# One fused attention and mixer kernel: batch 0's values cast whole into the hidden tile's space, its opening chain redealt over the engines, and batch 1's loads held back

## The chip, the core and the metric

The kernel runs on one core of a Trainium2 chip. Its time is the device time of one execution in microseconds, and lower is better. Five engines work side by side on a core: TensorE (PE in the profile) multiplies matrices, VectorE (DVE) and ScalarE (ACT) do element-wise work, GpSimd (POOL) does some casts and issues part of the DMA transfers, and SyncE (SP) issues the other transfers. Each engine runs its instructions in the order in which the program lists them, and semaphores hold an instruction until what it needs is there.

## The reference

The first half is a linear attention whose features are a ReLU times a cosine and a sine of the position. The second half is a mixer with a low-rank token part and a wide channel part.

```python
# q, k, v: (8 batches, 8 heads, 576 positions, 64)
phi(x) = concatenate([relu(x) * cos_w, relu(x) * sin_w], axis=-1)   # 128 features
kv  = einsum('bhsf,bhsd->bhfd', phi(k), v)
z   = sum(phi(k), axis=2)
num = einsum('bhsf,bhfd->bhsd', phi(q), kv)
den = einsum('bhsf,bhf->bhs', phi(q), z)[..., None] + 1e-06
x   = (num / den), heads side by side           # (8, 576, 512)
h   = x.transpose(0, 2, 1) @ U @ V              # U: 576 x 32, V: 32 x 576
u   = x + h.transpose(0, 2, 1)
out = u + relu(u @ w_ch1) @ w_ch2               # 512 -> 2048 -> 512
```

## The kernel before

The 576 positions of a batch lie in five chunks, `c` = 0 to 4: four of 128 positions and a tail of 64. Inputs come in as 32-bit floats (`qst`, `kst`, `vst`, one set for all batches) and are cast to bf16 for TensorE. The order of all work is written out by hand, engine by engine; nothing is planned by a scheduler. From the second batch on, attention work is dealt into slots beside the channel matmuls of the batch before. Batch 0 has nothing to hide behind, and its opening is the part that the change touches.

**The opening of batch 0** goes as follows. SyncE loads q, k and v of batch 0, then q of batch 1 into the same staging tiles as soon as they have been read, then k and v of batch 1. GpSimd loads U and V, the four slices of `w_ch1` (`w1_load`, L98) and later those of `w_ch2` (`w2_load`, L104). TensorE runs matmuls on zeros first (`keep_warm`, L195), then transposes q's features (`qtr_mm`, L366), sums k's features to z (`z_mm`, L892, one column for each head), and enters `first_chain` (L942).

**`first_chain`** works in two halves of four heads. VectorE has cast v to bf16 into `v_ext` (`v_block`, L278), and GpSimd the tail of v into `v_tl`. `kv_unit` (L315) multiplies k's features with v, with 65 columns for each head, the last one a column of ones. ScalarE casts its result to `kv`. `den_mm` (L900) makes the denominators from z, one column for each chunk and head, and `recip` (L402) inverts them on VectorE. `xh_mm` (L911) makes the numerators of one chunk and four heads, and `xh_norm` (L920) multiplies them on VectorE with the inverse and writes `x_bf`, or `x_tl` for the tail. `a_mm` (L436) makes the low-rank product `A` in two halves, each from four heads, and ScalarE casts both. `open_mm` (L935) and `uTd_mm` (L529) build the transposed u in four blocks, and `uTd_evac` (L526) casts each to `uT`. The first channel matmuls (`g1_main`, L541) read `uT` and `w_ch1`; slice n of `w_ch1` holds the columns of units 4n to 4n + 3.

**Around it.** The program text from L989 to L1037 issues the opening. `g1_main(0, j, True)` for j = 0 to 2 does half of the first three channel units. The slots follow: sixteen `g1_main` units of batch 0 (L794), beside them batch 1's q features and transposes, then the k features (`k_prep`, slots 9 to 13) and the v casts of batch 1 on VectorE (slot 15). After them come the `g2_part` units (L605), whose matmuls of part p read slice p of `w_ch2`, and beside the first two `kv_unit` of batch 1. A copy of one column of `vst` to `mark` (L1028) on GpSimd makes the `w_ch2` loads wait until a piece of batch 1's v has landed. A two-byte transfer of SyncE (`gate`, L1043, called at slot 15) makes the loads of batch 2 wait for slice 1 of `w_ch2`.

PSUM, where TensorE writes, is dealt by tags: `g` has three buffers, `T`, `oA`, `oB` one each, and `X` is a pair of banks. A buffer is free again when the last instruction that reads it is done. In `first_chain` the tile `xz` of tag `X` holds z, the denominators and both halves of `A`, and the fourth block of the transposed u takes the same tag after them. `hid` is the tag of the 16 x 512 hidden tile (L543), which is written first by ScalarE after the first channel unit.

Of the kernel before, what the change touches and what calls it, by code (L numbers as in the profile page):

```python
# [17 lines left out]
def kernel(  # L18
# [11 lines left out]
    nc = tc.nc  # L30
# [99 lines left out]
    for h0 in (0, 4):  # L130
        load_odd(vst, v, 0, h0, h0 + 4)
        load_even(vst, v, 0, h0, h0 + 4)
    def load_uv():
        nc.gpsimd.dma_start(out=stV, in_=moe_V)
        nines_u = moe_U.rearrange("(m k) r -> m (k r)", k=9)
        nc.gpsimd.dma_start(
            out=stU[:, 0:4, :].rearrange("p c r -> p (c r)"),
            in_=bass.AP(
                tensor=nines_u.tensor, offset=nines_u.offset,
                ap=[[9 * R, TS], [5 * R, 2], [1, 4 * R]],  # L140
            ),
        )
        for lo in (0, TS):
            nc.gpsimd.dma_start(out=stU[lo : lo + TS, 4, :], in_=nines_u[:, 4 * R : 5 * R])
# [130 lines left out]
            else:  # L275
                cast(eng, vx[tail(b), 4, h0:h1, 0:D], vst[tail(b), h0:h1, 4, :])

    def v_block(b, h0, h1, c0, c1, eng):  # L278
        cast(
            eng,  # L280
            v_ext[b % 2][:, c0:c1, h0:h1, 0:D].rearrange("p c h d -> p h c d"),
            vst[:, h0:h1, c0:c1, :],
        )

    def scaled_relu(eng, o, i, w):
        if eng is nc.scalar:
            nc.scalar.activation(out=o, in_=i, func=AF.Relu, bias=0.0, scale=w)  # L287
# [27 lines left out]
    def kv_unit(b, hg, tag, bufs, eng=None):  # L315
        if b not in kv_sb:
            kv_sb[b] = pool.tile([P, H, E], BF16, tag="kv", bufs=2, name="kv")
        acc = bank([P, 4, E], FP32, tag, bufs, "kv_ps")
        vx = v_ext[b % 2]
        for i in range(4):  # L320
            h = hg * 4 + i
            for c in range(5):
                nc.tensor.matmul(  # L323
                    out=acc[:, i, :],
                    lhsT=k_p[b][:, c, h, :] if c < 4 else k_tl[:, h, :],
                    rhs=v_tl[:, h, :] if c == 4 and b < 2 else vx[:, c, h, :],
                    start=(c == 0),
                    stop=(c == 4),
                )
        cast(eng or V_, kv_sb[b][:, hg * 4 : hg * 4 + 4, :], acc)  # L330

    def kv_pair(b, tag, bufs):
        kv_sb[b] = pool.tile([P, H, E], BF16, tag="kv", bufs=2, name="kv")
# [58 lines left out]
    def qT_of(b, c, h):  # L392
        return q_pT[b][:, c, h, :] if c < 4 else q_tlT[:, h, :]
# [495 lines left out]

    z_sb = const.tile([P, H], BF16)  # L890

    def z_mm(b, c, z):  # L892
        for h in range(H):
            nc.tensor.matmul(
                out=z[:, h : h + 1], lhsT=k_p[b][:, c, h, :] if c < 4 else k_tl[:, h, :],
                rhs=v_tl[:, 0, D:E], start=(c == 0 and h == 0),
                stop=(c == 4 and h == H - 1),
            )

    def den_mm(b, h0, h1, d_ps):  # L900
        for c in range(5):
            for h in range(h0, h1):
                nc.tensor.matmul(
                    out=d_ps[:, c, h - h0 : h - h0 + 1],
                    lhsT=qT_of(b, c, h),
                    rhs=z_sb[:, h : h + 1],
                    start=True,
                    stop=True,
                )

    def xh_mm(b, c, h0, tag, bufs):  # L911
# [8 lines left out]
    def xh_norm(b, c, h0, rec, acc):  # L920
        x_alloc(b)
        rows = slice(0, P) if c < 4 else tail(b)
        nc.vector.tensor_tensor(
            out=x_of(b, c, rows)[:, h0 * D : h0 * D + 4 * D].rearrange(
                "p (i d) -> p i d", d=D
            ),
            in0=acc[rows],
            in1=rec[rows, c, :].unsqueeze(2).to_broadcast([P if c < 4 else TS, 4, D]),
            op=ALU.mult,
        )  # L930

# [7 lines left out]
                start=(c == 0), stop=False,  # L939
            )  # L940

    def first_chain(b, xz, v_ps):  # L942
        z = xz[:, 0, 0:H]
        d = [
            xz[:, 0, H + 20 * i : H + 20 * i + 20].rearrange("p (c h) -> p c h", h=4)
            for i in range(2)
        ]
        rec = [pool.tile([P, 5, 4], FP32, tag="rec5", bufs=2, name="rec5") for _ in d]
        for h0 in (0, 4):
            v_block(b, h0, h0 + 4, 0, 4, V_)  # L950
        cast(V_, V_bf, v_ps.rearrange("r (c p) -> r c p", c=4))
        cast(A_, z_sb, z)
        kv_unit(b, 0, *T1, A_)
        den_mm(b, 0, 4, d[0])
        recip(rec[0], d[0])
        x0 = [xh_mm(b, c, 0, *t) for c, t in zip(ORD, (G3, G3, G3, OA, OB))]
        den_mm(b, 4, 8, d[1])
        kv_unit(b, 1, *T1, A_)
        for n in range(2):
            xh_norm(b, ORD[n], 0, rec[0], x0[n])  # L960
        recip(rec[1], d[1])
        for n in range(2, 5):
            xh_norm(b, ORD[n], 0, rec[0], x0[n])
        x1 = [xh_mm(b, c, 4, *t) for c, t in zip(ORD[0:4], (G3, G3, G3, OA))]
        for n in range(2):
            xh_norm(b, ORD[n], 4, rec[1], x1[n])
        uT_alloc(b)
        a_ps = xz[:, 1, 0:P]
        a_mm(b, a_ps, (0, 1), range(5))
        cast(A_, A_of(b)[0:TS, :], a_ps[0:TS, :])  # L970
        x1.append(xh_mm(b, ORD[4], 4, *G3))
        for n in range(2, 5):
            xh_norm(b, ORD[n], 4, rec[1], x1[n])
        for i, (tag, bufs) in enumerate((T1, OB, OA)):
# [3 lines left out]
        uTd_mm(b, 0)  # L978
        uTd_evac(b, 0, A_)
        uTd_mm(b, 1)  # L980
        uTd_evac(b, 1, V_)
        a_mm(b, a_ps, (2, 3), range(5))
        cast(A_, A_of(b)[TS:P, :], a_ps[TS:P, :])
# [30 lines left out]

    v_prep(0, 0, 4, (4,), (G_,))
    w1_load(0)
    v_prep(0, 4, 8, (4,), (G_,))
    for n in range(1, 4):
        w1_load(n)
    first_chain(0, xz, v_ps)  # L1020
    load_odd(qst, q, 1)
    load_even(qst, q, 1)
    load_odd(kst, k, 1)
    load_even(kst, k, 1)
    for h0 in (0, 4):
        load_odd(vst, v, 1, h0, h0 + 4)
        load_even(vst, v, 1, h0, h0 + 4)
    G_.tensor_copy(out=mark, in_=vst[0:TS, 3, 4, 0:1])  # L1028
# [108 lines left out]
```

## Time and profile before

| what | value |
|---|---|
| median of 3 runs | 298.73 us (298.7 to 298.75) |
| the profiled execution's own time | 298.44 us |
| its span, first to last instruction | 296.7 us |
| TensorE busy | 290.1 us |
| VectorE busy | 183.8 us |
| ScalarE busy | 158.1 us |
| GpSimd busy | 73.4 us |

The span starts with the first instruction of the program, and all times inside the trace are counted from there. The profiled execution is 0.29 us under the median of the runs, and 1.74 us of its time lie outside its span. TensorE is busy almost throughout; its matmuls are pipelined, so the durations of single matmuls overlap, and the chain of waits shows what each stretch of them adds to the end.

### The profile page before, as it was taken

How to read it: one execution, taken by the hardware profiler on the slowest of the kernel's cores; microseconds unless marked ns; L12 is line 12 of the kernel's file. 1: busy time of each engine (PE TensorE's matmuls, PEld its weight loads, DVE VectorE, ACT ScalarE, POOL GpSimd, SP SyncE). 2: the span in 40 equal slices, each digit the busy share in tenths (PEclk: the TensorE clock that was granted, in tenths of full speed). 3: DMA queues.
4: the chain of work that ended last, by engine and by line, in shares of the span. 5: the costliest groups of instructions: out<-in, count | busy, mean ns of one | idle time of the engine just before them, and what ended most of it. 6: DMA issues, size and time to landing. Idle time of an engine off the chain costs nothing.

```text
span 296.7 us, 7055 instructions
## 1 busy us (share of the span) xinstructions
PE 290.1 (98%) x2948; PEld 195.1 (66%) x2948; DVE 183.8 (62%) x359; ACT 158.1 (53%) x269; POOL 73.4 (25%) x113
## 2 busy tenths in 40 slices
PE   8999999999999999999999999999999999999994
PEld 6775455545987547854887547855887547845982
DVE  4898748887884668738734687538734586404341
ACT  2835561476693467745692457746692453067300
POOL 8340500050053305540051500540051101300130
PEclk9999999999999999999999999999999999999999
DMA  7999999999949994999999808996375104030004
GB/s 205 352 273 255 226 186 261 291 232 236 287 82 164 266 357 106 251 241 269 232 163 226 325 2 198 177 310 187 73 129 171 38 2 88 8 136 2 0 15 165
DMA packets 85281, 53.30 MB, mean 180 GB/s; under 512 B 54018, under 2 KB 82978, under 8 KB 85250
## 3 DMA queue, kind: packets, MB, share of 16 engines
q1 hardware_dynamic: 78802, 41.40, 59.0%
q0 software_dynamic: 6368, 11.43, 15.6%
q8 instruction: 23, 0.38, 0.5%
q14 instruction: 8, 0.07, 0.1%
q10 hardware_dynamic: 80, 0.03, 0.0%
HBM read 36.86 MB, written 9.44 MB: 156 GB/s over the span
## 4 chain that ended last, share of the span: by engine, by line
PE 95%; DMA 2%; ACT 1%; DVE 0%; issue 0%; ACTq 0%
PE g_ps L551 38%; PE w_ps L729 29%; PE gt_ps L571 5%; PE o_ps L611 5%; PE ot_ps L638 5%; PE x_ps L413 3%; PE kv_ps L339 2%; DMA qst<-in_q_dram 2%; PE w_ps L198 1%; PE va_ps L464 1%; PE a_ps L439 1%; PE kv_ps L323 1%; PE t_ps L368 1%; PE t_ps L356 1%; PE xh_ps L914 1%; PE va_ps L484 0%
## 5 line engine op out<-in xcount | busy, mean ns | idle before, releaser
L560 ACT ACTIVATE hid<-g_ps 128x512 bf16<-128x512 f32 x128 | 76.1, 597 | 85.1 <-PE g_ps L551 58.4
L551 PE MATMUL g_ps<-uT,w_bf 128*128 128x512 bf16 x512 | 120.8, 379 | 0.0
L551 PEld LDWEIGHTS <-w_bf 128*128 128x128 bf16 x512 | 46.3, 98 | 48.8 <-issue 0.2
L741 POOL TENSOR_TENSOR o_sb<-w_sum,u_bf 128x512 f32<-128x512 f32 x21 | 26.4, 1283 | 124.0 <-DVE w_sum L741 124.0
L729 PEld LDWEIGHTS <-hid 128*128 128x128 bf16 x448 | 43.6, 98 | 5.6
L729 PEld LDWEIGHTS <-S 128*128 128x128 bf16 x336 | 32.6, 98 | 4.1 <-DVE S L697 0.2
L741 DVE TENSOR_TENSOR o_sb<-o_sb,w_ps 128x512 f32<-128x512 f32 x28 | 19.2, 686 | 17.5 <-PE w_ps L729 11.1
L729 PE MATMUL w_ps<-w_bf,hid 128*128 128x256 bf16 x224 | 26.9, 273 | 0.0
L729 PE MATMUL w_ps<-T,hid 128*128 128x256 bf16 x224 | 26.7, 273 | 0.0
L729 PE MATMUL w_ps<-T,S 128*128 128x256 bf16 x224 | 26.0, 273 | 0.0
L473 DVE TENSOR_TENSOR u_bf<-x_bf,va_ps 128x1024 bf16<-128x1024 bf16 x16 | 19.3, 1216 | 7.2 <-PE va_ps L464 7.2
L114 POOL CAST v_ext<-vst 128x512 bf16<-128x512 f32 (+1 forms) x30 | 19.3, 678 | 13.2 <-DMA vst<-in_v_dram 12.8
L423 DVE TENSOR_TENSOR x_bf<-x_ps,rec 128x512 bf16<-128x512 f32 x28 | 19.4, 691 | 1.0
L697 DVE TENSOR_TENSOR S<-hid 128x1024 bf16<-128x1024 bf16 x14 | 9.7, 693 | 15.3 <-ACT hid L560 15.3
L403 DVE TENSOR_SCALAR rec<-x_ps 128x8 f32<-128x8 f32 (+1 forms) x35 | 5.7, 164 | 20.1 <-PE x_ps L413 20.0
L287 ACT ACTIVATE k_p<-kst,sinw 128x512 bf16<-128x512 f32 x26 | 17.1, 712 | 0.2 <-DMA kst<-in_k_dram 0.2
L585 POOL DMA_DIRECT2D out_dram<-o_sb x12 | 7.6, 630 | 38.3 <-DVE o_sb L619 21.4
L114 DVE CAST kv<-kv_ps 128x520 bf16<-128x520 f32 (+1 forms) x8 | 5.1, 632 | 17.5 <-PE kv_ps L339 13.9
L611 PE MATMUL o_ps<-w_bf,hid 128*128 128x512 bf16 x64 | 15.6, 379 | 0.0
L571 PEld LDWEIGHTS <-w_bf 128*128 128x128 bf16 x256 | 14.7, 98 | 0.9
L571 PE MATMUL gt_ps<-uT_tl,w_bf 128*128 128x128 bf16 x256 | 15.3, 219 | 0.0
L638 PE MATMUL ot_ps<-w_bf,hid_tl 128*128 128x512 bf16 (+2 forms) x80 | 15.0, 336 | 0.0
(145 smaller groups left out, 366.2 us busy)
## 6 DMA issues: line engine op xcount, KB each, us to landing
qst<-in_q_dram SPq DMA_DIRECT2D x14, 512.0 KB, 6.2
kst<-in_k_dram SPq DMA_DIRECT2D x14, 512.0 KB, 9.1
vst<-in_v_dram SPq DMA_DIRECT2D x12, 512.0 KB, 8.2
out_dram<-o_sb POOLq DMA_DIRECT2D x12, 512.0 KB, 6.7
w_bf<-in_moe_w_ch_dram POOLq DMA_DIRECT2D x8, 512.0 KB, 10.6
out_dram<-o_sb SPq DMA_DIRECT2D x4, 512.0 KB, 3.0
qst<-in_q_dram SPq DMA_DIRECT2D x2, 640.0 KB, 7.0
kst<-in_k_dram SPq DMA_DIRECT2D x2, 640.0 KB, 10.8
```

The lines of the kernel that those rows point to most:

```text
L114: eng.tensor_copy(out=o, in_=i)
L287: nc.scalar.activation(out=o, in_=i, func=AF.Relu, bias=0.0, scale=w)
L423: nc.vector.tensor_tensor(out=x_of(b, c, rows).rearrange("p (g i d) -> p g i d", g=2, d=D), in0=view[:, :, :, 0:D], in1=rec[rows].unsqueez ...
L473: nc.vector.tensor_tensor(out=u_bf[b][:, d0 : d0 + 2], in0=x_bf[b].rearrange("p c (d n) -> p d c n", n=P)[:, d0 : d0 + 2], in1=va_ps[b, d0 ...
L551: nc.tensor.matmul(out=g_ps.rearrange("p (c t) -> p c t", c=4), lhsT=w1_bf[:, d, j * P : j * P + P], rhs=uT[b][:, d, :, :], start=(d == 0) ...
L560: nc.scalar.activation(out=hid[b][:, j, :], in_=g_ps, func=AF.Relu, bias=0.0, scale=1.0)
L571: nc.tensor.matmul(out=g_ps[:, jj, :], lhsT=w1_bf[:, d, j * P : j * P + P], rhs=uT_tl[pr][:, d, :], start=(d == 0), stop=(d == 3),)
L611: nc.tensor.matmul(out=o, lhsT=hid[0][:, j, cc * P : cc * P + P], rhs=w2_bf[:, j, :], start=(j == 0), stop=(j == NJ - 1),)
L638: nc.tensor.matmul(out=o[:, cols], lhsT=hid_tl[pr][:, j, :], rhs=w2_bf[:, j, cols], start=(j == 0), stop=(j == NJ - 1),)
L697: V_.tensor_tensor(out=o, in0=a, in1=b_, op=op)
L729: nc.tensor.matmul(out=res[:, g, :], lhsT=lhs[:, k_, g * P : g * P + P], rhs=rhs[:, k_, :], start=(opens and k_ == 0 and g == 0), stop=(k_ ...
L741: eng.tensor_tensor(out=o, in0=x, in1=y, op=ALU.add)
```

## The change

v of batch 0 is cast as it lies, chunks and tail together, into a bf16 tile `v0` that takes the space of tag `hid`. `kv_unit` reads it for batch 0 and makes 64 columns instead of 65. z gets 48 equal columns for each head, and the denominators 12 equal columns for each chunk and head; one of them is read afterwards. The chain has all denominators in one piece and one inversion of 40 columns.

Work moves between engines: the sine feature of k's tail goes from ScalarE to VectorE, the tail of v from GpSimd to VectorE, the cast of `V_bf` from VectorE to ScalarE, the second half of `A` from ScalarE to VectorE, one of the ten normalisations to ScalarE (four activations of 64 columns), block 1 of `uT` to ScalarE and block 2 stays on VectorE. The cast of the q tail's transpose (`qtr_evac(0, 4)`) comes after the first two pieces of v. The second half of `A` and some other results lie in other PSUM buffers. The blocks 2 and 3 of the transposed u are closed before the first channel matmuls. Some matmuls on zeros go, and three of 384 columns come in (`fill`).

The order of loads: slice 0 of `w_ch1` waits for a piece of batch 0's v, slices 1 to 3 for batch 0's first `kv`. Batch 1's k, and behind it on the same queue batch 1's v, wait for the same `kv` by a two-byte transfer on SyncE. `w_ch2` waits for batch 1's k instead of its v.

```diff
+    v0 = pool.tile([P, H, 5, D], BF16, tag="hid", bufs=1, name="v0")
...
     def kv_unit(b, hg, tag, bufs, eng=None):
-        acc = bank([P, 4, E], FP32, tag, bufs, "kv_ps")
+        n = D if b == 0 else E
+        acc = bank([P, 4, n], FP32, tag, bufs, "kv_ps")
...
-                    rhs=v_tl[:, h, :] if c == 4 and b < 2 else vx[:, c, h, :],
+                    rhs=(
+                        v0[:, h, c, :] if b == 0
+                        else v_tl[:, h, :] if c == 4 and b < 2 else vx[:, c, h, :]
+                    ),
...
+    ones = const.tile([P, 48], BF16)
+    V_.memset(ones, 1.0)
...
-                out=z[:, h : h + 1], lhsT=k_p[b][:, c, h, :] if c < 4 else k_tl[:, h, :],
-                rhs=v_tl[:, 0, D:E], start=(c == 0 and h == 0),
+                out=z[:, h, :], lhsT=k_p[b][:, c, h, :] if c < 4 else k_tl[:, h, :],
+                rhs=ones, start=(c == 0 and h == 0), stop=(c == 4 and h == H - 1),
...
+                    out=d[:, c, h, :], lhsT=qT_of(b, c, h),
+                    rhs=z_sb[:, h : h + 1].to_broadcast([P, 12]), start=True, stop=True,
...
+    def xh_norm_act(b, c, h0, rec, acc):
+        x_alloc(b)
+        rows = slice(0, P) if c < 4 else tail(b)
+        for i in range(4):
+            nc.scalar.activation(
+                out=x_of(b, c, rows)[:, (h0 + i) * D : (h0 + i) * D + D],
+                in_=acc[rows, i, :], func=AF.Copy, bias=0.0,
+                scale=rec[rows, c, h0 + i : h0 + i + 1],
+            )
...
+    def first_chain(b, xz, z, v_ps):
+        def fill(n):
+            for _ in range(n):
+                nc.tensor.matmul(
+                    out=xz[:, 1, P:512], lhsT=zero[:, 0:P], rhs=zero[:, 0:384],
+                    start=True, stop=True,
+                )
+
+        d = xz[:, 1, 0:480].rearrange("p (c h n) -> p c h n", h=H, n=12)
+        rec = pool.tile([P, 5, H], FP32, tag="rec5", bufs=1, name="rec5")
+        fill(1)
+        for h in (0, 2):
+            cast(V_, v0[:, h : h + 2], vst[:, h : h + 2])
+        qtr_evac(b, 4, V_, t_q[4])
+        cast(V_, v0[:, 4:H], vst[:, 4:H])
+        cast(A_, z_sb, z[:, :, 0])
+        kv_unit(b, 0, *G3, A_)
+        cast(A_, V_bf, v_ps.rearrange("r (c p) -> r c p", c=4))
+        den_mm(b, d)
+        recip(rec, d[:, :, :, 0])
         x0 = [xh_mm(b, c, 0, *t) for c, t in zip(ORD, (G3, G3, G3, OA, OB))]
-        den_mm(b, 4, 8, d[1])
         kv_unit(b, 1, *T1, A_)
+        fill(2)
+        xh_norm_act(b, ORD[4], 0, rec, x0[4])
+        for n in range(4):
+            xh_norm(b, ORD[n], 0, rec, x0[n])
+        x1 = [xh_mm(b, c, 4, *t) for c, t in zip(ORD[0:4], (G3, G3, G3, T1))]
...
+        for i in range(2):
+            uTd_mm(b, i)
+            uTd_evac(b, i, A_)
+        a2 = bank([P, P], FP32, *G3, "a_ps")
+        a_mm(b, a2, (2, 3), range(5))
+        cast(V_, A_of(b)[TS:P, :], a2[TS:P, :])
...
-    keep_warm(2, *T1)
     for c in TL:
-        k_prep(0, c, (V_, A_))
-        keep_warm(2 if c < 2 else 1, *T1)
-        z_mm(0, c, xz[:, 0, 0:H])
-        if c == 1:
-            qtr_evac(0, 4, V_, t_q[4])
-    v_ps = spread_v(*OB)
+        k_prep(0, c, (V_, A_ if c < 4 else V_))
+        if c < 3:
+            keep_warm((1, 2, 1)[c], *T1)
+        if c == 3:
+            v_ps = spread_v(*T1)
+        z_mm(0, c, z)
...
-    v_prep(0, 0, 4, (4,), (G_,))
+    G_.tensor_copy(out=mark, in_=vst[0:TS, 3, 4, 0:1])
     w1_load(0)
-    v_prep(0, 4, 8, (4,), (G_,))
+    first_chain(0, xz, z, v_ps)
+    G_.tensor_copy(out=mark[0:1], in_=kv_sb[0][0:1, 0, 0:1])
     for n in range(1, 4):
         w1_load(n)
-    first_chain(0, xz, v_ps)
     load_odd(qst, q, 1)
     load_even(qst, q, 1)
+    nc.sync.dma_start(out=mark2, in_=kv_sb[0][0:1, 0, 0:1])
     load_odd(kst, k, 1)
     load_even(kst, k, 1)
...
-    G_.tensor_copy(out=mark, in_=vst[0:TS, 3, 4, 0:1])
+    G_.tensor_copy(out=mark, in_=kst[0:TS, 3, 4, 0:1])
     for n in range(4):
         w2_load(n)
-    g1_main(0, 0, True)
     uTd_close(0, 2, V_)
     uTd_close(0, 3, A_)
-    g1_main(0, 1, True)
-    g1_main(0, 2, True)
+    for j in range(3):
+        g1_main(0, j, True)
```

More of the change, by code (lines that the diff above doesn't have):

```diff
@@ L276, in v_prep @@
                 cast(eng, vx[tail(b), 4, h0:h1, 0:D], vst[tail(b), h0:h1, 4, :])
[L278 to L283, printed above, removed]
     def scaled_relu(eng, o, i, w):
@@ L329, in kv_unit @@
                 )
-        cast(eng or V_, kv_sb[b][:, hg * 4 : hg * 4 + 4, :], acc)
+        cast(eng or V_, kv_sb[b][:, hg * 4 : hg * 4 + 4, 0:n], acc)
     def kv_pair(b, tag, bufs):
@@ L927, in xh_norm @@
             in0=acc[rows],
-            in1=rec[rows, c, :].unsqueeze(2).to_broadcast([P if c < 4 else TS, 4, D]),
+            in1=rec[rows, c, h0 : h0 + 4].unsqueeze(2).to_broadcast([P if c < 4 else TS, 4, D]),
             op=ALU.mult,
@@ L940, in open_mm @@
             )
[L942 to L955, printed above, removed]
+    def xh_norm_act(b, c, h0, rec, acc):
[7 more added lines that the diff above has]
+            )
@@ L972, in first_chain @@
         for n in range(2, 5):
-            xh_norm(b, ORD[n], 4, rec[1], x1[n])
-        for i, (tag, bufs) in enumerate((T1, OB, OA)):
+            xh_norm(b, ORD[n], 4, rec, x1[n])
+        for i, (tag, bufs) in enumerate((OA, OB, T1)):
             uT_ps[b, i] = bank([P, 4, P], FP32, tag, bufs, "uT_ps")
```

26 lines of the change are left out of this document (5 added, 21 removed).

## The prediction

> **What bounds the kernel now.** I read the last chain first, then the windows, then the chain in order of time.
>
> ```profile
> PE 95%; DMA 2%; ACT 1%; DVE 0%; issue 0%; ACTq 0%
> ...
> 24.00:40.00 16.00, 16.00 (x117) 8.29 (x116) 13.25 (x27) 10.97 (x21) 4.50 (x9) 1.00 1.11 224
> ```
>
> From 24 us on TensorE is busy in all 16.00 us of the window, at a granted clock of 1.00, and the chain stays on it to the end. The change touches the opening, so its worth is how much earlier the dense stream of channel matmuls gets going, less what the stream has to wait later. This is the stretch:
>
> ```profile
> 15.90 0.71 PE kv_ps L323 x20
> 16.61 0.48 PE xz L903 x20
> 17.09 0.77 PE xh_ps L914 x20
> 17.86 0.48 PE xz L903 x20
> 18.34 0.66 PE kv_ps L323 x20
> ...
> 19.01 0.40 ACT kv L112
> ...
> 19.45 0.66 PE xh_ps L914 x16
> 20.11 0.39 PE xz L439 x10
> 20.50 0.23 PE xh_ps L914 x4
> 20.73 0.45 PE uT_ps L937 x8
> 21.18 0.37 PE uT_ps L531 x2
> 21.55 0.59 ACT uT L112
> ...
> 22.16 0.28 ACT A_sb L112
> ...
> 22.48 0.38 PE u L937 x4
> 22.86 0.43 PE g_ps L551 x2
> ...
> 25.45 0.45 PE t_ps L356 x8
> ```
>
> The rows are start, duration and work. The chain leaves TensorE at three places: ScalarE's cast of the second `kv` (19.01), its cast of `uT` (21.55), and its cast of `A` (22.16), for which the last transposes wait because they take over the buffer `xz`. Ten channel matmuls and the closing of blocks 2 and 3 then fill 22.86 to 25.45, 2.59 us. My mark is that 25.45, where the next work, batch 1's first transpose, begins.
>
> **Part by part: up to the first kv.**
>
> ```profile
> 11.82 2.56 ACT L287 ACTIVATE k_p<-kst,sinw 128x512 bf16<-128x512 f32 x4 [0.24 <-DMA kst<-in_k_dram]
> 11.84 0.88 DVE L289 TENSOR_SCALAR k_p<-kst,cosw 128x512 bf16<-128x512 f32 x2
> ...
> 12.64 0.68 DVE L114 COPY q_tlT<-t_ps 128x512 bf16<-128x512 bf16 x1
> ...
> 13.24 1.02 DVE L289 TENSOR_SCALAR k_p<-kst,cosw 128x512 bf16<-128x512 f32 x2
> ...
> 14.57 1.68 DVE L114 CAST v_ext<-vst 128x1024 bf16<-128x1024 f32 x2
> ```
>
> VectorE steps through k's features at 0.40 us each (11.84 to 12.64 for two). It now has six in a row, the tail's sine included: 11.84 + 2.40 = 14.24. Two v casts of 1024 elements take 1.68 us with a tail of 0.08, so 0.80 each; a piece of 640 costs 0.50 and the piece of 1280 1.00. The first pieces are there at 14.82 and 15.32. Then the q tail's copy (0.60, from 12.64 to 13.24) to 15.84 and the last piece to 16.84. The second pair of k casts took 1.02 us where the first took 0.88; GpSimd's v casts, which ran in that time, are gone, so I count 0.40 for all. The Trainium skill, "SBUF — State Buffer", section "SBUF: two separate sides", says that such a VectorE cast and a GpSimd instruction lock each other out of a shared port pair; the pair of 0.88 and 1.02 agrees, and without this rule the step would end 0.14 later.
>
> ScalarE ends its four k features at 14.38, and z's matmuls follow. 48 columns in place of one cost TensorE at most what 64-column matmuls do (0.77 for 20 against 0.48), so 0.12 more for a chunk, inside ScalarE's step of 0.64 per chunk; only the last chunk's shows. `kv_unit` 0 can finish when the second piece is there, 15.32 plus half of 0.71: 15.68, against 16.61 before.
>
> **Denominators and numerators.** 40 denominator matmuls cost 0.96 at the one-column price and 1.54 at the 64-column price. 12 is nearer to one; I take 0.96, to 16.64, and keep 0.58 for the range. ScalarE casts `kv` (0.40, to 16.1) and `V_bf` (0.59 like `uT`, to 16.7) beside them. The five numerators (0.77) end at 17.41 and `kv_unit` 1 (0.66) at 18.07; its v was there at 16.92. ScalarE's second cast ends at 18.5. The fills stand in this wait and cost nothing unless `kv` comes sooner than they end (two of 384 columns, 0.33 by the 0.45 for 1024 columns of transposes). The second numerators start at 18.55 instead of 19.45.
>
> **Norms and A.**
>
> ```profile
> 17.20 0.18 DVE L403 TENSOR_SCALAR rec<-xz 128x20 f32<-128x20 f32 x1 [0.36 <-PE xz L903]
> 17.41 0.28 DVE L404 RECIPROCAL rec<-rec 128x20 f32<-128x20 f32 x1
> ...
> 20.12 1.40 DVE L923 TENSOR_TENSOR x_bf<-xh_ps,rec 128x256 bf16<-128x256 f32 x4
> ```
>
> Inverting 40 columns costs 0.28 to 0.56; I take 0.42, with 0.2 for the addition: VectorE is free at 16.84, so 17.5. Norms step at 0.33 (1.40 for four), so four end at 18.8 and those of the second half run from there to about 20.2; the last needs its numerator.
>
> ScalarE takes one norm as four scaled activations of 64 columns. `A` (128 columns) took 0.28 and `uT` (512) 0.59, so 64 columns are about 0.23; k's scaled ones step at 0.64 against 0.59. I count 0.26 each, 1.04 in all, with bounds of 0.20 and of 0.40 (the 260-column `kv`): 18.5 to 19.55. The first `A` waits for this chunk, and its last four matmuls (0.15) end at 19.75 instead of 20.50. Then the last numerator (0.23) to 19.98, eight transposes (0.45) to 20.43, two closes (0.37) to 20.80. ScalarE casts both `uT` blocks, 0.59 each: 21.4 and 21.95. The last norm ends at 20.4, so the second `A` runs on TensorE from 20.80 to 21.19, VectorE casts it (0.28) to 21.5 while blocks 2 and 3 are opened (0.45) to 21.65. It lies in a buffer of its own and ScalarE doesn't cast it: the wait at 22.16 is gone. Closes and ten channel matmuls (2.59) end at 24.24; `uT` 1 at 21.95 is needed just after the closes (0.32), at 21.97. **Opening: 24.24 against 25.45, 1.2 us earlier.**
>
> **The loads.**
>
> ```profile
> 14.41 0.60 SPq L78 DMA_DIRECT2D kst<-in_k_dram  x1
> ...
> 19.70 2.13 SPq L72 DMA_DIRECT2D vst<-in_v_dram  x1
> ...
> 33.09 0.18 POOL L1028 COPY mark<-vst 64x1 f32<-64x1 f32 x1 [15.05 <-DMA vst<-in_v_dram]
> ...
> 37.96 1.42 DVE L114 CAST v_ext<-vst 128x512 bf16<-128x512 f32 x4
> ...
> 40.28 1.03 PE L611 MATMUL o_ps<-w_bf,hid 128*128 128x512 bf16 x4
> ...
> 41.14 0.29 PE L323 MATMUL kv_ps<-v_ext,k_p 128*128 128x65 bf16 x4
> ```
>
> The sources' own rows have issue and landing: the four `w_ch1` slices, the four `w_ch2` slices, that last v load alone, and q's loads of batches 0 and 1.
>
> ```profile
> L100 POOL DMA_DIRECT2D w_bf<-in_moe_w_ch_dram x4: 750/836/960, 14.0 to 17.3; - x4
> ...
> DMA to landing us min/median/max: 8.4/13.0/18.3
> ```
> ```profile
> L106 POOL DMA_DIRECT2D w_bf<-in_moe_w_ch_dram x4: 747/756/851, 33.2 to 35.4; - x4
> ...
> DMA to landing us min/median/max: 5.7/9.1/12.6
> ```
> ```profile
> DMA to landing us min/median/max: 16.4/16.4/16.4
> ```
> ```profile
> L72 SPq DMA_DIRECT2D qst<-in_q_dram x2: 602/621/640, 1.7 to 11.0; - x2
> ...
> DMA to landing us min/median/max: 6.3/7.0/7.7
> ```
>
> `w_ch1` landed from 22.4 to 35.6: 4.4 us a slice while it shared the DMA engines with k and v. `w_ch2` landed from 38.9 to 48.0: 3.0 a slice, mostly alone. v's last load landed at 36.1, and q's last of batch 1 at up to 18.7 (11.0 and 7.7).
>
> Slice 0 is issued 0.3 earlier, because a short copy replaces a cast, and has some 2 us without k, worth 2 x (1 - 3.0/4.4) = 0.6: it lands near 21.5, and the first channel matmul wants it at 21.97. Slices 1 to 3 are issued from 16.4 on, 0.8 later than before, but queue behind it, so they land some 0.9 earlier and the stream, 1.2 earlier, keeps most of its margin. If `kv` came later, each us would go into them first.
>
> k is issued at about 16.8 instead of 14.41: `kv` is there at 16.1, and a two-byte transfer is issued first on SyncE (some 0.60, like k's own issue). All of v stands behind k. q of batch 1 fills that queue until shortly before it lands, so the loss is 1 to 2.4 us. `w_ch2` starts at about 29 instead of 33.1 and shares with v's end, which had the engines nearly to itself. I put v's last landing at 37.4 to 38.5. VectorE's v casts take 1.8 (1.42 and one more of about 0.4): done at 39.2 to 40.3. `kv_unit` of batch 1 ran at 41.14 and now wants them at 39.94: a wait of 0 to 0.4. Slice 0 of `w_ch2` comes a shared 4.4 behind `w_ch1`'s end at 34.7, at 38.3 to 39.1, for matmuls that ran at 40.28 and now want it at 39.1. I take 0.1 for both, with 0.8 as the upper bound. What follows (slice 1 of `w_ch2`, the gate of batch 2's loads) comes earlier than before.
>
> **Sum.** 1.2 - 0.1 = 1.1 us off the profiled 298.44: 297.34. The median of the runs stood 0.29 above that execution, so 297.6. The unknown prices add up to 1.3 on the bad side (0.58 denominators, 0.56 activations, 0.14 inversion) and 0.4 on the good one, and the loads to 0.7, not all at once: the forecast's own range is 297.1 to 298.4.
>
> **Rivals.**
>
> *ScalarE becomes the bound.* It gets `V_bf`, four activations and one `uT` block more (0.59 + 1.04 + 0.59) and loses a feature (0.64) and an `A` cast (0.28). For it: the chain already leaves TensorE three times, each time for ScalarE. Against: it idles between these casts. With 0.40 for each activation and the dear denominators, 1.1 of the 1.2 goes: 298.6.
>
> *Batch 1's v comes too late.* One mechanism: the hold on k pushes v, and `w_ch2`, released by k, takes half of the engines from it. It decides from a last landing after 39.3 (41.14 less 1.8): then `kv_unit` runs later than before and the opening's gain is lost. For it: v's margin was only 41.14 - 1.8 - 36.1 = 3.2, and the full 2.4 of the hold plus 1 to 2 us of sharing exceed it. Against: q's remainder covers part of the hold. A landing at 40.3 gives +1.0: 299.7.
>
> *The clock falls.* The trace shows one slow start:
>
> ```profile
> 1.19 7.63 PE L198 MATMUL w_ps<-zero 128*128 128x512 bf16 x76 [1.19 <-DVE zero L123]
> ```
>
> 4 matmuls of 512 and 72 of 128 columns, 11264, take 7.63 us where the transposes' rate (1024 in 0.45) gives 4.95. Fewer matmuls on zeros between k's chunks could bring that back. Doubling TensorE's pieces from 18.34 to 22.86 (3.1 us) gives 300.7. The Trainium skill, "TensorE: Matmul & The Clock Gate", section "Part 1: The HAM clock gate", says that an idle window of about 3.4 us halves the clock; my steps leave no gap above 0.5 us, so by it this stays unlikely.
>
> *The hold does nothing*, k being behind q anyway: slice 0 comes at 22.1 and the first matmul with it, 0.1 later: 297.8.
>
> **Chances.** Forecast 0.60, ScalarE 0.15, late v 0.14, clock 0.08, idle hold 0.03. About 0.6 us (0.2%) is what a measurement can tell from no change. Faster: 0.57 of the forecast, 0.04 of ScalarE, 0.04 of late v, all of the idle hold: 0.68. Same: 0.03, 0.09 and 0.03: 0.15. Slower: 0.02, 0.07 and 0.08: 0.17. The range of 296.9 to 299.2 leaves out 0.04 below and 0.15 above.
>
> **What would show it.** Right: the second `kv` cast starts near 18.1, the second `A` is cast by VectorE before ScalarE is done with `uT`, batch 1's first transpose starts at 24.0 to 24.5, and TensorE has no gap from 38 to 42. Wrong: scaled activations over 0.35 us each, denominators over 1.3 us, a first channel matmul that waits for `w_ch1`, `kv_unit` of batch 1 waiting for v's casts, or a granted clock under 1.00 after 6 us.

## The result, and the profile after

The changed kernel takes 297.11 us (median of four, 296.75 to 297.40) against 298.72; the ratio is 0.9945 with a 95% interval of 0.9928 to 0.9963. Run again later beside the experiments it took 297.80 (ratio 0.9961, 0.9946 to 0.9977). The profiled execution took 296.9 us with a span of 295.1. Medians are over all executions, while the ratios leave out those that took over 1.5% more than the fastest of their kernel, so a ratio need not be the quotient of two medians.

From the page after, the shares of the chain that ended last, by engine:

```profile
PE 98%; DVE 0%; ACT 0%; issue 0%
```

The 2% of DMA that stood in this chain before, q's load, are gone: the chain now goes back over TensorE's matmuls on zeros, and TensorE is on it nearly all the way. The opening, in the chain of waits after (start, duration, work):

```profile
14.70 0.17 PE xz L953
14.87 0.58 PE kv_ps L319 x20
15.45 0.78 PE xz L904 x32
16.23 0.06 issue
16.30 0.36 PE xz L904 x8
16.65 0.63 PE xh_ps L912 x20
17.28 0.60 PE kv_ps L319 x20
...
17.90 0.40 ACT kv L112
...
18.34 0.81 PE xh_ps L912 x16
19.15 0.39 PE xz L438 x10
19.54 0.23 PE xh_ps L912 x4
...
20.54 0.48 PE a_ps L438 x10
...
21.89 2.26 PE g_ps L550 x10
24.16 0.45 PE t_ps L355 x8
```

Of the three places where the chain left TensorE, one is left, the cast of the second `kv`. The casts of `uT` and `A` are no longer on it, and ten channel matmuls run in one piece instead of two and eight. The mark, batch 1's first transpose, moved from 25.45 to 24.16: 1.29 us.

The windows after (start and end, length, then the busy times of PE, PEld, DVE, ACT and POOL, the granted clock and the DMA share) show TensorE without a gap, and the last matmuls in the chain show that the gain is there at the end:

```profile
20.00:24.00 4.00, 4.00 (x37) 2.01 (x35) 3.04 (x9) 2.53 (x5) 0.00 (x0) 1.00 1.16 233
24.00:40.00 16.00, 16.00 (x120) 8.32 (x119) 11.67 (x23) 11.14 (x22) 4.51 (x9) 1.00 1.18 254
```
```profile
287.48 3.51 PE ot_ps L637 x32
```

The same last matmuls started at 288.76 before, so 1.28 of the 1.6 us between the spans came from the opening; the other 0.3 lie behind the last matmul. The rows of the `w_ch1` loads, to set beside those of before:

```profile
L100 POOL DMA_DIRECT2D w_bf<-in_moe_w_ch_dram x4: 750/779/1532, 13.6 to 18.0; - x4
...
  PEld L550: 0.2, 1
...
DMA to landing us min/median/max: 8.2/11.4/16.9
```

Slice 0 of `w_ch1` is issued at 13.57 and lands at 21.72 (22.44 before). The weight load of the first channel matmul waited 0.2 us for it, while TensorE was still at other work. Slice 0 of `w_ch2` is issued at 31.47 and lands at 38.98.

### The profile page after: what moved, and what is told of

The parts are those of the page before. It is cut to its first block, busy times and chain, and to the rows that moved or that the text cites. A ratio compares the mean times of both kernels' runs of the same rounds, so it can differ in the third digit from the quotient of the medians.

```text
span 295.1 us, 7056 instructions
## 1 busy us (share of the span) xinstructions
PE 289.5 (98%) x2946; PEld 194.9 (66%) x2946; DVE 182.7 (62%) x358; ACT 159.1 (54%) x273; POOL 72.2 (24%) x113
## 4 chain that ended last, share of the span: by engine, by line
PE 98%; DVE 0%; ACT 0%; issue 0%
PE g_ps L550 38%; PE w_ps L728 29%; PE gt_ps L570 5%; PE o_ps L610 5%; PE ot_ps L637 5%; PE w_ps L200 3%; PE x_ps L412 3%; PE kv_ps L338 2%; PE a_ps L438 1%; PE va_ps L463 1%; PE kv_ps L319 1%; PE t_ps L355 1%; PE t_ps L367 1%; PE xh_ps L912 1%; PE va_ps L483 0%; PE xz L904 0%
## 5 line engine op out<-in xcount | busy, mean ns | idle before, releaser
L114 POOL CAST v_ext<-vst 128x512 bf16<-128x512 f32 (+1 forms) x30 | 17.9, 635 | 12.0 <-DMA vst<-in_v_dram 11.6
```

Source lines behind the costliest of these rows:

```text
L114: eng.tensor_copy(out=o, in_=i)
```

## The experiments

Twelve kernels ran, in three groups of four, each group beside the kernel before (medians 298.81, 298.81 and 298.89). Each ran twelve times, but for loads as before (ten), k held longer (five) and one column with more warm-up (six). The mark, the start of batch 1's first transpose, is read from the chain of waits of one profiled execution, and landings are of that execution too.

| run | slice 0 of `w_ch1` lands | mark | median, us | ratio, 95% interval |
|---|---|---|---|---|
| changed kernel again | 21.74 | 24.12 | 297.80 | 0.9961 [0.9946, 0.9977] |
| loads as before | 24.02 | 26.40 | 300.19 | 1.0047 [1.0018, 1.0075] |
| loads alone | 21.12 | 25.72 | 299.14 | 1.0007 [0.9981, 1.0034] |
| k held longer | 21.20 | 23.94 | 297.15 | 0.9937 [0.9918, 0.9956] |
| k not held | 24.20 | 27.49 | 300.59 | 1.0032 [0.9992, 1.0071] |
| slices not gated | 21.56 | 24.32 | 297.15 | 0.9949 [0.9917, 0.9981] |
| one column | 20.92 | 26.31 | 297.68 | 0.9951 [0.9924, 0.9978] |
| one column, more warm-up | 21.08 | 24.48 | 297.44 | 0.9957 [0.9943, 0.9972] |
| `A` shared | 21.05 | 25.49 | 297.89 | 0.9961 [0.9940, 0.9983] |
| fifth norm on VectorE | 21.83 | 24.48 | 297.66 | 0.9961 [0.9947, 0.9975] |
| no fills | 22.09 | 24.47 | 298.23 | 0.9970 [0.9938, 1.0002] |
| `kv` first | 20.96 | 24.44 | 297.65 | 0.9964 [0.9947, 0.9981] |

The chain passes by the mark of the last two; theirs is the transposes' start in the timeline plus the 0.17 by which the chain's start lies behind it in the changed kernel (23.99 against 24.16). The mark varies between executions: for the changed kernel and three kernels whose opening chain was expected to be no slower (k held longer, slices not gated, one column with more warm-up) it lies between 23.94 and 24.48. So steps of 0.3 us are read from the rows in front of the mark.

### The two parts of the change, each alone

The changed kernel again:

> The changed kernel once more. Theory 1 (k's landing): its runs spread (296.75 to 297.4 us) because the shorter chain is now bound by ScalarE's four k features, which start when batch 0's k lands; in the first trace they start at 11.50 us and batch 1's first transpose at 24.16, and where they start at 11.8 it should be 24.4 to 24.5 and the time about 0.3 us higher. Theory 2 (the clock): the spread comes from when the granted clock rises during the matmuls on zeros (6.8 us in the first trace), and k's landing changes nothing. Median by both: 296.8 to 297.4.

The chain of after with the loads of before:

```diff
-    w1_load(0)
+    for n in range(4):
+        w1_load(n)
     first_chain(0, xz, z, v_ps)
-    G_.tensor_copy(out=mark[0:1], in_=kv_sb[0][0:1, 0, 0:1])
-    for n in range(1, 4):
-        w1_load(n)
...
-    nc.sync.dma_start(out=mark2, in_=kv_sb[0][0:1, 0, 0:1])
     load_odd(kst, k, 1)
...
-    G_.tensor_copy(out=mark, in_=kst[0:TS, 3, 4, 0:1])
+    G_.tensor_copy(out=mark, in_=vst[0:TS, 3, 4, 0:1])
```

> The chain of the change with the order of loads of before: all four slices of w_ch1 behind the v mark, k of batch 1 not held, w_ch2 released by batch 1's v. If the hold on k matters (theory 1): slice 0 of w_ch1 lands at 22.2 to 22.5 instead of 21.7, the first channel matmul waits for it, and batch 1's first transpose comes at 24.6 to 24.9 instead of 24.16: 0.4 to 0.7 us slower than the change, about 297.6. If the chain alone makes the gain (theory 2): as the change within 0.2 us, about 297.1.

And the reverse, the chain of before with the gates and releases of after (the same lines, put into the kernel before; slice 0 still stands behind the first cast of v's tail, as it does there):

> The chain of before with the order of loads of the change alone. Both theories: the chain is not bound by loads before 22.8 us, so batch 1's first transpose stays at 25.4 to 25.5 and the time within 0.2 us of before (298.5 to 298.9). The rival that the late v costs: kv_unit of batch 1 waits for v's casts at 41 us and the time is 299 or more, since the first kv, and with it k, comes 0.8 us later than in the change.

In the changed kernel run again k of batch 0 landed at 11.16, 0.26 earlier than in its first profile, and the mark moved by 0.04 only. Its chain of waits says why:

```profile
13.26 8.48 DMA w_bf<-in_moe_w_ch_dram
21.74 0.05 issue
21.78 2.33 PE g_ps L550 x10
```

In this execution slice 0 set the mark. The weight load waited 0.4 us for it, and the first channel matmul started 0.46 behind the start of the last closes (21.32 to 21.78 in the timeline), where 0.32 lie between them in the first profile (21.50 to 21.82). So the load cost about 0.15 us there, the changed kernel has hardly any slack for it, and what an earlier k is worth stays open.

Neither part gains alone. With the new chain and the old loads the kernel is slower than before by 0.2 to 0.8%. The first theory has the right cause and the wrong size: it put slice 0 at 22.2 to 22.5 and the time near 297.6. From the chain of waits:

```profile
14.12 9.90 DMA w_bf<-in_moe_w_ch_dram
...
24.07 2.33 PE g_ps L550 x10
26.40 0.45 PE t_ps L355 x8
```

The chain runs through slice 0, issued at 14.12 and landed at 24.02; TensorE waits 2.0 us for it. With the old chain and the new loads slice 0 is there at 21.12, but the channel matmuls start at 23.14: that kernel keeps TensorE's waits for the casts of `kv` (0.5) and `A` (0.3), and its time is that of before (299.14, a little over the 298.5 to 298.9 expected).

### Which gate does it

```diff
-    nc.sync.dma_start(out=mark2, in_=kv_sb[0][0:1, 0, 0:1])
```

> Only the hold on batch 1's k is taken out; slices 1 to 3 of w_ch1 still wait for kv. Theory A (k's transfers, issued from about 14.4 us, take the DMA engines before slice 0 of w_ch1 has its first packet): slice 0 lands at 23.5 to 24.2 instead of 21.7, the first channel matmul waits 1.8 to 2.3 us for it, batch 1's first transpose starts at 26.0 to 26.5, time 298.9 to 300.3. Theory B (slices 1 to 3, issued right behind slice 0, share the engines with it): slice 0 lands at 21.2 to 22.0 as in the changed kernel, that transpose at 24.0 to 24.5, time 296.9 to 297.6.

```diff
-    w1_load(0)
+    for n in range(4):
+        w1_load(n)
     first_chain(0, xz, z, v_ps)
-    G_.tensor_copy(out=mark[0:1], in_=kv_sb[0][0:1, 0, 0:1])
-    for n in range(1, 4):
-        w1_load(n)
```

> Only the gate on slices 1 to 3 of w_ch1 is taken out: all four are issued back to back, while batch 1's k stays held. Theory A (k delays slice 0): slice 0 lands at 21.2 to 21.9, batch 1's first transpose starts at 24.0 to 24.5, time 296.9 to 297.6. Theory B (slices 1 to 3 share the engines with slice 0): slice 0 lands at 23 or later, the first channel matmul waits over 1 us, batch 1's first transpose at 25.4 or later, time 298.3 or more.

Theory A holds, theory B falls. From the chain of waits and the source's view of the run without the hold:

```profile
13.61 10.59 DMA w_bf<-in_moe_w_ch_dram
...
24.25 3.24 PE g_ps L550 x10
27.49 0.85 PE t_ps L355 x8
```
```profile
  PEld L550: 2.9, 1
  PE g_ps L550: 2.6, 1
```

Slice 0 is issued at 13.61, where the changed kernel issues it at 13.57, and lands 2.5 us later. The one difference in the kernel is k, issued at 14.13 and 14.83 instead of 16.75 and 17.49: the first packet of slice 0 moves at 17.99 instead of 16.42. What the queues moved from 16.4 to 18.0 (packets, MB, and the time of the packets as a share of the 16 engines' time, which can pass 100%; q0 carries GpSimd's loads, q1 SyncE's), first in the changed kernel, then without the hold:

```profile
q0 software_dynamic: 198, 0.20, 82.6%
q1 hardware_dynamic: 170, 0.19, 36.0%
```
```profile
q1 hardware_dynamic: 536, 0.56, 108.0%
q0 software_dynamic: 1, 0.00, 0.4%
```

Without the hold SyncE's queue fills the engines in this stretch, and slice 0 moves next to nothing. Slices issued right behind slice 0 cost it next to nothing (13.03 to 21.56, 8.5 us against 8.2).

One thing does not fit a plain "k ahead of slice 0". The kernel before does not hold k either (issued at 14.41 and 15.12, slice 0 at 13.99), and there the first packet of slice 0 moves at 16.59, nearly as early as with the hold. One difference shows in the rows: GpSimd's issuing instruction of slice 0 took 0.96 us there and ended at 14.95, just before SyncE's first issuing instruction of k did (15.01). It took 1.53 without the hold and with the loads as before, and ended at 15.14 and 15.65, behind that of k (14.73 and 15.24). Whether this order decides was not tried, so the hold is shown to be needed with the new chain as it stands, and not for every kernel with a free k.

And there is a second price, by which the mark (27.49) and the time go beyond what theory A had. The ten matmuls behind the wait took 3.24 us instead of 2.26; the windows (busy times, the granted clock third from the end) show why:

```profile
25.00:26.00 1.00, 1.00 (x5) 0.35 (x4) 0.00 (x0) 0.00 (x0) 0.00 (x0) 0.76 1.17 244
26.00:27.00 1.00, 1.00 (x4) 0.43 (x3) 0.00 (x0) 0.32 (x1) 0.20 (x2) 0.50 1.17 264
...
28.00:29.00 1.00, 1.00 (x7) 0.47 (x5) 0.61 (x2) 0.13 (x1) 1.00 (x2) 0.53 1.17 247
```

The wait is 2.6 us long, and the clock is granted at half from about 25.5 to 28.9 (0.76 and 0.53 are mixtures). The executions of this run fall into two groups: six with a mean clock of 0.996 or more took 298.29 to 299.59 us; six at 0.987 to 0.992 took 301.58 to 302.85. So even with the clock up (median 299.0) this kernel is not faster than the one before. The groups' medians lie 3.1 us apart, and half of 3.4 us is 1.7, so by this estimate the clock is not all of that difference; one execution, of the slower group, was profiled.

### Holding k longer

```diff
-    nc.sync.dma_start(out=mark2, in_=kv_sb[0][0:1, 0, 0:1])
+    nc.sync.dma_start(out=mark2, in_=kv_sb[0][0:1, 4, 0:1])
```

> The change with batch 1's k held until the second kv cast (about 18.3 us) instead of the first (15.9), 2.4 us later. The prediction's rival of a late v: v's last landing moves from 36.9 by 1 to 2.4 us to 38 to 39.3, its casts end 1.8 later at 39.8 to 41.1, and kv_unit of batch 1, which wants them at 39.9, waits 0 to 1.2 us: 297.2 to 298.4. The other view, that w_ch1 ends earlier by as much as k comes later, so that v has the DMA engines to itself at the end: v's landing moves by under 1 us and the time stays within 0.2 us of the change.

k is issued 2.3 us later (19.07), and nothing waits for it: v's last landing is 35.68, no later than in the two profiles of the changed kernel (36.94 and 35.84). Slices 1 to 3 are done by 32.70, where the changed kernel's first profile has them by 34.84, so v has less beside it at the end. The time is that of the changed kernel. A held load here is work put off behind other work on the same engines, and v's end shows none of the 2.3 us.

### Columns as warm-up

```diff
-    ones = const.tile([P, 48], BF16)
+    ones = const.tile([P, 1], BF16)
...
-                    rhs=z_sb[:, h : h + 1].to_broadcast([P, 12]), start=True, stop=True,
+                    rhs=z_sb[:, h : h + 1], start=True, stop=True,
```

> z is summed in one column instead of 48 and the denominators in one instead of 12; all else is the changed kernel. Theory (the columns cost next to nothing on the path and only keep TensorE busy): 40 denominator matmuls take 0.9 to 1.0 us as before against 0.96, batch 1's first transpose starts within 0.2 us of 24.1, time within 0.6 us of the changed kernel's. Rival (the columns are paid for): z ends earlier, the denominators are 0.2 us shorter or more, that transpose starts at 23.6 to 23.9 unless slice 0 of w_ch1 is late. Rival (the columns hold the clock): with fewer of them the granted clock falls below 1.00 between 8 and 16 us and the chain starts 0.5 us later or more, time 297.6 or more.

And with both of these edits and, beside them:

```diff
+    keep_warm(2, *T1)
...
-            keep_warm((1, 2, 1)[c], *T1)
+            keep_warm((2, 2, 1)[c], *T1)
+        else:
+            nc.tensor.matmul(
+                out=xz[:, 1, 0:512], lhsT=zero[:, 0:P], rhs=zero[:, 0:512], start=True, stop=True
+            )
```

> As in the run with one column each for z and the denominators, with the matmuls on zeros between k's chunks put back to the numbers that the kernel before has (two ahead, then two, two, one, one, one). Theory (the equal columns are warm-up in another form: what held the clock in the changed kernel is the work that TensorE streams in 11 to 16 us, whichever matmul does it): the granted clock stays at 1.00 from 8 to 24 us, batch 1's first transpose starts at 23.9 to 24.5, time 296.6 to 297.5. Rival (one-column matmuls themselves lower the clock, or the fall came from k landing late in that execution): the clock falls again below 0.9 somewhere in 12 to 24 us where k lands after 11.6 us, and that transpose starts after 25.5, time over 298.

Windows of the profiled execution with one column and the changed kernel's few warm-ups:

```profile
12.00:13.00 1.00, 0.35 (x9) 0.32 (x10) 1.00 (x3) 1.00 (x2) 0.00 (x0) 1.00 1.09 356
...
14.00:15.00 1.00, 1.00 (x26) 0.74 (x25) 1.00 (x3) 1.00 (x2) 1.00 (x1) 0.91 1.08 354
15.00:16.00 1.00, 1.00 (x19) 0.83 (x16) 1.00 (x3) 0.52 (x2) 0.47 (x1) 0.50 1.07 360
...
21.00:22.00 1.00, 1.00 (x20) 0.73 (x18) 0.96 (x3) 0.17 (x1) 0.00 (x0) 0.68 1.19 231
```

The clock was halved from 14.8 to 21.6, and the mark came at 26.31. k landed at 11.79 here, 0.37 later than in the changed kernel, and the longest wait of TensorE was 0.7 us. Late k alone does not do it: in the run with the shared `A` k landed at 12.26 and in the run with `kv` first at 12.13, with the wide columns in both. The window of the latter's wait is emptier, and the clock stays:

```profile
12.00:13.00 1.00, 0.01 (x1) 0.01 (x1) 0.77 (x2) 0.78 (x2) 0.00 (x0) 1.00 1.10 357
```

The fall did not come in every execution: of the twelve with one column two had a mean clock of 0.989 (299.01 and 299.44 us), and four at 1.00 took 296.31 to 297.47. With more warm-ups all six executions kept 0.998 or more. This points to wide columns standing in for matmuls on zeros, and does not show it. Two falls in twelve would leave six executions without one about a third of the time by chance, the medians of the two forms (297.68 and 297.44) are alike, and in the profiled execution with more warm-ups k was early (11.14), so this form was not seen under a late k. The columns' price is plain: 40 denominators took 0.98 us with one column there.

### Single steps of the chain

```diff
-        a2 = bank([P, P], FP32, *G3, "a_ps")
-        a_mm(b, a2, (2, 3), range(5))
-        cast(V_, A_of(b)[TS:P, :], a2[TS:P, :])
+        a_mm(b, a_ps, (2, 3), range(5))
+        cast(A_, A_of(b)[TS:P, :], a_ps[TS:P, :])
```

> The second A goes back into the shared buffer xz and is cast by ScalarE behind its uT casts, as in the kernel before; all else is the changed kernel. Theory (a buffer of its own and VectorE's cast removed a wait of ScalarE's 0.28 us): the chain shows an A cast by ScalarE again, the last transposes and batch 1's first transpose start 0.2 to 0.5 us later (24.3 to 24.6), time 297.1 to 297.6. Rival (channel matmuls fill that wait and slice 0 of w_ch1 sets the stream anyway): batch 1's first transpose within 0.1 us of the changed kernel's 24.16, no difference in time.

From the chain of waits:

```profile
17.28 0.63 PE xh_ps L912 x20
...
21.10 1.07 ACT uT L112 x2
22.20 0.28 ACT A_sb L112
...
25.49 0.45 PE t_ps L355 x8
```

This execution began late (k at 12.26), so the mark is measured from the first numerators: 8.21 us, against 7.51 in the changed kernel. In this execution the buffer of its own with VectorE's cast is worth 0.7, more than both readings expected: ScalarE casts two `uT` blocks (1.07) ahead of `A` now, where it cast one before. The times (297.89 against 297.80) don't tell the two apart, though 0.7 us should show there; why it doesn't stays open.

```diff
-        xh_norm_act(b, ORD[4], 0, rec, x0[4])
-        for n in range(4):
+        for n in range(5):
             xh_norm(b, ORD[n], 0, rec, x0[n])
```

> The fifth norm of the first half goes back to VectorE; ScalarE's four scaled activations are gone. Theory (the last norm sets the second A): VectorE's norms end 0.33 us later, near 21.0 by the changed kernel's 20.68, the second A's matmuls and its cast follow, batch 1's first transpose starts 0.15 to 0.35 us later than 24.16 when measured against the first numerators' start. Rival (ScalarE's 0.92 us was on the path, as the first A waits for that chunk): the first A starts 0.05 us or more earlier and that transpose too. Either way under 0.4 us, so the times alone (297.0 to 297.6) will hardly tell.

VectorE's rows of this run in the timeline:

```profile
19.27 0.41 DVE L921 TENSOR_TENSOR x_tl<-xh_ps,rec 64x256 bf16<-64x256 f32 x1
19.60 1.40 DVE L921 TENSOR_TENSOR x_bf<-xh_ps,rec 128x256 bf16<-128x256 f32 x4
```

The norms end at 21.00; the changed kernel's last row of them, of the same length, starts at 19.28 and ends at 20.68. The mark follows by the same 0.32, about as the theory had it (0.36 from the first numerators, which started 0.04 earlier). The path is partly another one. From the chain of waits, behind VectorE's norms:

```profile
19.34 0.34 DVE x_tl L921
...
19.73 0.29 PE xh_ps L912 x4
```

The last numerators, at 19.73 instead of 19.54, already start late behind VectorE's norms, and the second `A`, which takes 0.56 instead of 0.48, adds to it. ScalarE's norm takes a step off VectorE, and VectorE sets both.

```diff
-        fill(1)
...
-        fill(2)
```

> The three fills on zeros in the chain are taken out. Theory (the one ahead of kv stands on the path with its 0.17 us, since v's first piece is there when it starts; the two ahead of the second numerators stand inside the wait for ScalarE's cast): kv_unit 0 starts right behind z, everything behind it up to 0.17 us earlier, the wait for the second kv cast 0.33 us longer, the granted clock 1.00, time within 0.3 us of the changed kernel's. Rival (the fills hold the clock): the granted clock falls under 1.00 in 14 to 24 us, time 298 or more. Rival (v's piece is not there): kv_unit 0 starts at the same time, nothing gained.

From the chain of waits:

```profile
15.96 0.28 issue
16.25 0.33 PE xz L904 x7
```
```profile
16.16 0.83 DVE L114 CAST v<-vst 128x1280 bf16<-128x1280 f32 x1 [0.95 <-DMA vst<-in_v_dram]
```

`kv_unit` 0 did start right behind z (14.57), but 0.28 us of a wait that the profile gives no cause for ("issue") came up among the denominators. It ends at 16.25, as the changed kernel's 0.06 ends at 16.30. And VectorE could not have used an earlier start: it waits for batch 0's v until 16.16 (16.13 in the changed kernel) and starts the norms at 17.64 (17.61). So nothing was gained. The mark is 0.31 later, mostly because slice 0 landed at 22.09 and the first channel matmul waited 0.2 us for it. The clock stayed at 1.00 in this execution. v's last load landed at 38.85, the latest seen, and here it was met: the chain of waits runs through it and its casts to `kv_unit` of batch 1, which went on at 40.70. The median (298.23) is 0.43 above the changed kernel's, more than expected, in a wide spread (296.58 to 300.76).

### An attempt to go further

```diff
-        fill(1)
...
+        kv_unit(b, 1, *T1, A_)
         x0 = [xh_mm(b, c, 0, *t) for c, t in zip(ORD, (G3, G3, G3, OA, OB))]
-        kv_unit(b, 1, *T1, A_)
-        fill(2)
...
-    nc.sync.dma_start(out=mark2, in_=kv_sb[0][0:1, 0, 0:1])
+    nc.sync.dma_start(out=mark2, in_=kv_sb[0][0:1, 4, 0:1])
```

> An attempt to go further: batch 1's k is held for the second kv, the fills are out, and the second kv_unit runs ahead of the first numerators, so that its cast by ScalarE lies beside them. Theory (the cast of the second kv, 0.40 to 0.46 us without TensorE, is the one wait left in the chain): that wait is gone, the second numerators start behind the first ones when VectorE has given their buffers back, batch 1's first transpose starts at 23.5 to 23.8, time 296.3 to 296.9. Rival (VectorE's norms are the bound by then): the second half's norms end no earlier than 0.2 us before those of the run with the longer hold (20.46), and that transpose starts at 23.7 to 24.0, time 296.7 to 297.2. Rival (v's last cast is late): kv_unit 1 waits for it on TensorE and pushes the numerators back, that transpose at 24.1 or later.

The wait for the second `kv` cast is gone, and the gain is not there. From the end of the denominators (16.99) the norms take until 20.95, 3.96 us; in the run with k held longer it was 3.91 (16.55 to 20.46). VectorE is the bound by then, as the first rival says. The start was late for k, and it met a wait of the load side:

```profile
PE o_ps L610 <- DMA w_bf<-in_moe_w_ch_dram: 0.5, 1, 0.5
```

k, issued at 19.04 and 19.77, landed at 33.72 and released `w_ch2` only then. Its time (297.65) misses the 296.3 to 296.9 that the theory had. No version beat the changed kernel beyond the intervals.

## Why the prediction was right

The time and the cause were as forecast: the opening gains 1.29 us by the mark where the sum had 1.2, and the loads cost nothing where it had 0.1. The first 297.11 lies at the lower edge of the forecast's own range (297.1 to 298.4), the 297.80 of the second measurement near its middle, and the forecast was 297.6. The four signs named for a right forecast came: the second `kv` cast started at 17.90, VectorE had cast the second `A` by 21.34 and ScalarE the two `uT` blocks by 21.65, the mark was 24.16, and TensorE had no gap from 38 to 42.

**The steps held** within 0.3 us. `kv_unit` 0 ended at 15.45 (15.68 forecast), the second numerators started at 18.34 (18.55), the first `A` ended at 19.54 (19.75), the first channel matmul started at 21.89 (21.97). ScalarE's four scaled activations took 0.92 (1.04), the inversion 0.40 (0.42). 40 denominators of twelve columns took 0.98 where no stall came between (in the run without gated slices), as at the price of one column. In the changed kernel the last eight came later, and it was 1.20.

**Part of this is luck.** The steps were counted from k's first feature on VectorE at 11.84, and in the profile after, where batch 0's k landed 0.32 earlier (11.42 for 11.74), it started at 11.52. From there the opening took 12.64 us to the mark, where 12.40 were forecast and 13.61 were taken before: a gain of 0.97, and the earlier start would supply the rest of the 1.29, if all of the chain hangs on it. The second measurement's gain in time is 1.0 (298.81 to 297.80). Behind that sum two errors on VectorE cancel: it was put free at 16.84 and was free at 16.88, but its casts of v cost less (0.83 for the last piece instead of 1.00), and it waited 0.75 us for batch 0's v, a wait that the sum does not have.

**The loads.** v's last landing was put at 37.4 to 38.5 and came at 36.94; `w_ch2` was put at 38.3 to 39.1 and came at 38.98, although it was issued at 31.47 and not at about 29. The step took the hold on k for a pure loss to v. The run with k held longer shows that it is less: the channel slices finish earlier, and v catches up.

**What failed is the rival that the hold does nothing**, and the term behind it: "some 2 us without k, worth 2 x (1 - 3.0/4.4) = 0.6", with a price of 0.1 for the case without it. That reckoned with fair sharing from the moment of issue, and with the landing that the kernel before has without a hold. Measured in the new chain, the hold brings slice 0 forward by 2.5 us (24.20 to 21.72), and without it the kernel is no faster than before (ratio 0.9992 to 1.0071). The prediction credited the gain to the chain and booked the loads as a cost; the runs show that the redealt chain, as it is written, gains only with the hold.

**ScalarE as the bound** did not come. In the changed kernel's chain of waits one ScalarE cast of 0.40 is left, and where the chain leaves TensorE in the runs with the norm on VectorE, without fills and with `kv` first, it runs over VectorE's norms. **Late v** did not come in the changed kernel; 38.85, the worst landing seen, was under the threshold of 39.3, though it did make `kv_unit` wait there. **The clock** did not fall in the opening of the changed kernel's profiles. But the reason given (no gap above 0.5 us) was too weak: with narrow columns it fell with no wait above 0.7. The Trainium skill, "TensorE: Matmul & The Clock Gate", section "Part 1: The HAM clock gate", ties the fall to an idle window of about 3.4 us. The lengths agree, 3.4 us in the run without the hold and 6.8, twice that, with one column; that the window must be idle agrees with neither. Without the hold the wait was 2.6 us and TensorE worked again from 24.25, before the fall at 25.5; with one column its rows before the fall are 0.35 to 1.00 busy.

## What to carry to other kernels

Where a faster chain ends in work that needs a large load, look up when that load lands before counting the gain: here the same redealing gains about 1 us or nothing, by whether another queue's transfers start 2.6 us later or not. Price parts of a change together when one delivers what the other uses. Where columns cost nothing, as for the 40 denominators (0.98 us with one or twelve), useful matmuls can be made wide; that this keeps the clock is likely here and not shown. A load held behind others need not be later at its end.

## What was not expected of the hardware

The hold tells first on slice 0's first packet: it moved 2.9 us after the issue with k held (13.57 to 16.42) and 4.4 us after it with k free (13.61 to 17.99). From there to the landing it took 5.3 and 6.2. So about 1.5 of the 2.5 us are the first packet's, and most of the rest went by while the bytes moved. Whether k's queue keeps the engines or GpSimd's transfer is set up too late was not separated.

GpSimd's issuing instruction has two lengths. In the twelve profiles with the new chain it took 0.81 us for slice 0 in four (the changed kernel again, k held longer, slices not gated, norm on VectorE), where VectorE's first casts of v began behind it, and 1.53 in the other eight, where they began 0.3 us after its start. With k held the first packet moved between 16.37 and 16.66 with either length, whenever slice 0 was issued (12.84 to 14.41), while the landing that the traces give for batch 1's q lies between 16.96 and 17.55.

Without the hold the mean clock falls into two groups by the execution, and so does the time (298.3 to 299.6 and 301.6 to 302.9 us); in the one that was profiled a wait of 2.6 us stood ahead of the halved clock.

Some of the scatter of single executions has another source, far from the change. In the profiled execution with the norm on VectorE (mark 24.48, span 297.7) one transfer of a later batch took 12.24 us, and TensorE waited 1.9 us for it, by its chain of waits:

```profile
125.50 12.24 DMA q_pT<-q_p
...
137.79 0.43 PE x_ps L412 x8
```

So effects of 0.3 us can't be read from the times.
